# Two-layer recurrent attention on one core: first-step values, weight halves, transposes in steps 0, 1 and 67, and the order of the last dense tiles

## The chip, the cores and the metric

One core of a Trainium2 chip. The time is device microseconds for one execution of the program; the figure for a kernel is the median over its runs.

## The reference, cut to what matters

```python
def _A_ref(x, mem0, Wq, Wk, Wv, Wo, seg_len):     # S 2048, Dm 512, H 32, Dh 128, M 8, seg_len 32
    mem = mem0
    for s in range(n_seg):                        # 64 segments, each needs the memory of the one before
        xs = x[:, s * seg_len:(s + 1) * seg_len, :]
        h = concatenate([mem, xs], axis=1)        # 40 rows
        q, k, v = h @ Wq, h @ Wk, h @ Wv          # per head
        scores = where(mask, q @ k.T * scale, -1e9)
        o = (softmax(scores) @ v) @ Wo            # summed over heads
        mem = o[:, :M, :]
        outs.append(o[:, M:, :])
    return concatenate(outs, axis=1)

x = A_x
x = x + _A_ref(_layernorm(x), A_mem0, A_Wq, A_Wk, A_Wv, A_Wo, A_seg_len)
x = x + relu(_layernorm(x) @ B_w1) @ B_w2         # Dff 1376
x = x + _A_ref(_layernorm(x), A_mem0, A_Wq, A_Wk, A_Wv, A_Wo, A_seg_len)
x = x + relu(_layernorm(x) @ B_w1) @ B_w2
```

Both attention layers, and both dense layers, have the same weights. All arrays are bf16.

## The kernel before, in words

**Steps.** The work is cut into 68 steps (`LAST` = 67). Step k does segment k of the first attention layer (a = 0) and segment k - 4 of the second (a = 1, `DELTA` = 4), so that one load of a weight tile serves both layers. Steps 0 to 3 and 64 to 67 have one layer only. The two layers sit in partitions 0 to 39 and 64 to 103 of the score, P and value tiles.

**A step on TensorE (PE).** `qk(0)`: queries and keys of heads 0 to 15 (L467); scores of that half (L497); `qk(1)` and its scores for heads 16 to 31; P transposed, so that keys lie in partitions (first half: one DMA transpose, `turn_p`, or PE in `transpose_p`, L534); `weighted_v` (pv, L560); copies of pv into `OTm` (memory rows) and `OTx` (tokens), L577; `output_mem` (wo, L505), which gives the new memory; its copy wm, the transposes mt (L743) into `HT` and `HTm`; `memory_values` (vm, L636) for the next step. Work with no place in this chain fills gaps: `output_x(k - 1)`, the token outputs of the step before (wox, L327 with 64 rows, L348 with 32); the dense layer of tile d = k - 2 (`dense_h`, hp, L407; `dense_y`, sp, L427; `add_dense`; `store`); `values0`, the values of the next two segments of layer 0 (vp, L288, eight matmuls for each n of 0, 2, 4, 6); `values1` (L309). In steps with k % 4 == 0 ("ride" steps) the tokens of layer 0 go through the memory product in `OTm` and not through `OTx`.

**Values take a way through DRAM.** Heads have to move from the free dimension of a product into partitions of `Vs`; so values are written to DRAM (vst to vd, L297; VmS to vmd, L641) and read back (Vs<-vd, L620; Vs<-vmd, L646). In step 0 POOL's queue carries these DMAs, later SP's. A DMA that has to wait for another holds up all that stands behind it in its queue: in step 0 POOL has eight writes of vd, the read Vs<-vd, two writes of vmd, two reads Vs<-vmd, and behind these the multiply of the first half of P (L526).

**Order.** The orders of PE, VectorE (DVE), SP and POOL are the order in which the code records them (`manual_schedule`); high priority pulls the recurrent chain ahead. ScalarE's order is set by a scheduler.

**Start.** SP issues x0, x1, mem0, then the weights in quarters of 1 MB: Wq, Wk, Wq, Wk, Wv four times, Wq, Wk, Wq, Wk (L134) and Wo four times. Inputs are normalized (L219), transposed on PE (L230) and copied (L237). `HT` and `HTm` get the first memory at L772 and L773.

**End.** Segments 66 and 67 of layer 1 leave their rows in the second halves of tiles 66 and 67; dense tile 65 is done in step 67. Behind step 67 come `output_x(67)`, its adds (L362), the layer norm of the 128-row tile that holds both (bn_stats L786, normalize L219 into XN), its transposes (L230), the copy xnT (L790), hidden layer (hp), sums (sp), four adds (L798) and two DMAs.

**The clock.** PE's granted clock in the profile is 1.00 or 0.50.

Of the kernel before, what the change touches and what calls it, by code (L numbers as in the profile page):

```python
# [22 lines left out]
def kernel(  # L23
# [57 lines left out]
    def place1(s):  # L81
        if ride1(s):
            return s + 4, 32
        return s, (0 if s % 4 == 0 else 32)
# [23 lines left out]
    load_xb(1)  # L108
    nc.sync.dma_start(out=mem0[0:M, :], in_=A_mem0[0, :, :])
# [20 lines left out]
    PW = H * Dh // 4  # L130
# [4 lines left out]

    for pc in range(2):
        load_w(Wq_sb, Wq_v, pc)
        load_w(Wk_sb, Wk_v, pc)
    for pc in range(4):
        load_w(Wv_sb, Wv_v, pc)  # L140
    for pc in range(2, 4):
        load_w(Wq_sb, Wq_v, pc)
        load_w(Wk_sb, Wk_v, pc)
# [174 lines left out]
    def ox_span(k):  # L318
        offs = ([0] if has0(k) and not ride0(k) else [])
        if has1(k) and not ride1(k):  # L320
            offs.append(place1(k)[1])
        return (base(k) + min(offs), base(k) + max(offs) + 32) if offs else None
# [13 lines left out]
    def output_x(k, lo, hi):  # L336
        if not 0 <= k <= LAST or ox_span(k) is None:
            return
        r0, r1 = [x - base(k) for x in ox_span(k)]
        if lo == 0:  # L340
            pool, tag = (ps_wo, "wo") if k < LAST else (ps_fill, "fill")
            wo_tiles[k] = pool.tile([128, Dm], F32, tag=tag, name="wox")
        for h in range(lo, hi):
            if r1 - r0 == 64:
                halves(wo_tiles[k], OTx[:, h, r0:r1], Wo_sb[:, h, :], h == 0, h == H - 1)
            else:
                for j in range(4):
                    nc.tensor.matmul(wo_tiles[k][32 * j:32 * j + 32, 0:128], lhsT=OTx[:, h, r0:r1],  # L348
                                     rhs=Wo_sb[:, h, 128 * j:128 * j + 128], start=(h == 0), stop=(h == H - 1),
                                     tile_position=(0, 32 * j))  # L350
# [63 lines left out]
    def dense_y(d, f0, f1):  # L414
        if not 0 <= d <= LAST:
            return
        lo, hi = span(d)
        summed(d, f0, f1, hi - lo)

    def summed(d, f0, f1, n):  # L420
        for fc in range(f0, f1):
            fs = 128 if fc < NFC - 1 else F_LAST
            for j in range(2):


                w = 8 * L if fc == 0 else 256
                nc.tensor.matmul(sp_banks[1][64 * j:64 * j + n, 0:w], lhsT=hT_tiles[d][0:fs, fc, 0:n],  # L427
                                 rhs=w2_flat[0:fs, fc * Dm + 256 * j:fc * Dm + 256 * j + w],
                                 start=(fc == 0), stop=(fc == NFC - 1), skip_group_check=True, tile_position=(0, 64 * j))
# [71 lines left out]
    def output_mem(k, wo):  # L501
        n, c = divmod(k % 4, 2)
        for h in range(H):
            j = h % 4
            nc.tensor.matmul(wo[32 * j:32 * j + 32, :], lhsT=OTm[:, h, n, 2 * M * c:2 * M * c + 4 * M], rhs=Wo_sb[:, h, :],  # L505
                             start=(h < 4), stop=(h >= H - 4), tile_position=(0, 32 * j))

    def softmax(hf, act, meanwhile=lambda: None):
# [11 lines left out]
        meanwhile()  # L520
        for a, es in ess.items():
            sm = wk.tile([128, 8], F32, tag="sm", bufs=2)
            nc.vector.tensor_reduce(out=sm[:], in_=es[:], axis=AX.X, op=ALU.add)  # L523
            nc.vector.reciprocal(out=sm[:], in_=sm[:])  # L524
            eng = nc.vector if (hf, a) == (1, act[-1]) else nc.gpsimd
            eng.tensor_tensor(out=P_sb[:, :, 64 * a:64 * a + L], in0=es[:],  # L526
                              in1=sm[:].unsqueeze(2).to_broadcast([128, 8, L]), op=ALU.mult)
# [37 lines left out]
    def outputs(k, pvs):  # L565
# [7 lines left out]
        def copy(t, a, dst, lo, hi, parts=1):  # L573
            src = pvs[t, a][:, 0:PVS[t][1], lo:hi]
            if parts > 1:
                src = src.rearrange("p h (n t) -> p h n t", n=parts)
            engines[a if len(act) == 2 else t % 2](out=dst, in_=src)  # L577
# [16 lines left out]
        for a in act:  # L594
            for t in every:
                mem(t, a)
                if a == 0 and ride0(k):
                    quarter(t, 0)
            for t in every:
                if a == 0 and ride0(k):  # L600
                    quarter(t, 1)
                else:
                    tok(t, a)
# [47 lines left out]
    def block(k, lo, hi):  # L651
        output_x(k - 1, lo, hi)
        if k % 4 == 1 and has0(k + 1):
            p = (k + 1) // 2
            for n in range(0, NCH, 2):
                wo_bank = n == 0 or (n == 6 and k > 1)
# [4 lines left out]
    def step(k):  # L661
# [4 lines left out]
        has_x = n_x < NXT  # L666
        if k % 4 == 0 and has_x:
            load_xb(n_x)
# [7 lines left out]
        with tc.high_priority(offset=PRIO):  # L676
            load_values(k, act, q)
        if k == 0:
            with tc.high_priority(offset=PRIO):
                memory_values(0, q)  # L680
        part = 5 if len(act) == 2 else 8
        block(k, 0, part)
        with tc.high_priority(offset=PRIO):
# [3 lines left out]
            softmax(0, act)  # L687
            if k > 0:
                turn_p()
# [6 lines left out]
        if k == LAST - 2:  # L696
            for r in (0, 64):
                nc.gpsimd.memset(residual(LAST)[r:r + SEG, :], 0.0)
        with tc.high_priority(offset=PRIO):
            qks = qk(1, act)  # L700
        dense_h(k - 2)
        with tc.high_priority(offset=PRIO):
            scores(qks, act)
            if k == 0:
                softmax(1, act, lambda: transpose_p(0))
            else:
                softmax(1, act)
        block(k, part, 24 if k == 1 else H)
        ahead = has1(k + 1) or not cont
        f_mid = 9 if ahead else 5  # L710
        dense_y(k - 2, 0, f_mid)
# [5 lines left out]
        if ahead:  # L717
# [4 lines left out]
        with tc.high_priority(offset=PRIO):  # L722
            pvs = weighted_v(act)
            outputs(k, pvs)
            if cont:
                wo = ps_wo.tile([128, Dm], F32, tag="wo", name="wo")
                output_mem(k, wo)
                wm_sb = wm_tiles[k] = wk.tile([128, Dm], BF, tag="vst", bufs=5, name="wm")
                nc.scalar.copy(out=wm_sb[:], in_=wo[:])
        if k == 1:  # L730
            block(k, 24, H)
        if not ahead:
            dense_y(k - 2, f_mid, NFC)
        add_dense(k - 2)
        store(k - 2)
# [15 lines left out]
        if cont:  # L751
            output_ride(k)
            with tc.high_priority(offset=PRIO):
                memory_values(k + 1, nc.sync)
# [11 lines left out]
    with tc.manual_schedule(engines={mybir.EngineType.PE, mybir.EngineType.DVE, mybir.EngineType.SP,  # L766
# [14 lines left out]
        for k in range(LAST + 1):  # L781
            step(k)
        output_x(LAST, 0, H)
        add_output(LAST)
        R = residual(LAST)
        nc.vector.bn_stats(out=stats_all[:], in_=R[:])  # L786
        normalize(nc.vector, XN, R, stat_tail(stats_all), 0, 128)
        tp = transpose_pe(XN)
        xnT = wk.tile([128, NC4, 128], BF, tag="xnT", bufs=2, name="xnT")
        nc.scalar.copy(out=xnT[:], in_=tp[:])  # L790
        hidden(LAST, lambda c4: xnT[:, c4, :].rearrange("p (d t) -> p d t", d=2)[:, :, SEG:64], 64)
        summed(LAST, 0, NFC, 64)
        ob = wk.tile([128, Dm], BF, tag="ob", bufs=1, name="ob")
        for e in range(2):
            r = 64 * e + SEG
            for j in range(2):
                cs = slice(256 * j, 256 * j + 256)
                nc.vector.tensor_tensor(out=ob[r:r + SEG, cs], in0=R[r:r + SEG, cs],  # L798
                                        in1=sp_banks[1][64 * j + SEG * e:64 * j + SEG * e + SEG, 0:256], op=ALU.add)
            g = LAST - 1 + e - DELTA  # L800
            nc.sync.dma_start(out=out[0, SEG * g:SEG * g + SEG, :], in_=ob[r:r + SEG, :])
# [35 lines left out]
```

## Time and profile before

| what | value |
|---|---|
| median of 3 runs (1629.74, 1635.59, 1633.28) | 1633.28 us |
| profiled execution's own time | 1629.26 us |
| its span in the profile | 1627.5 us |
| granted PE clock, mean | 0.987 |
| PE busy / VectorE / ScalarE / POOL | 1569.9 / 1256.8 / 736.7 / 355.6 us |
| matmuls | 42966 |
| step 24 to step 63, each | 23.3 to 23.6 us, a few up to 0.7 longer |

The page has the busy time of each engine, the span in 40 slices (a digit is the busy share in tenths), the DMA queues, the chain of waits that ended last (shares by engine and by line), and the costliest groups of instructions. Each line of a timeline gives the start, the time, the engine, the line of the kernel, the operation with its tiles and shapes, the count of instructions run together, and in brackets the idle time before and what ended it.

### The profile page before, as it was taken

Reading aid. Unit: us, or ns where it says so; the run is one execution under the profiler, and the core shown is the slowest. Engines: PE = TensorE matmul, PEld = TensorE weight load, DVE = VectorE, ACT = ScalarE, POOL = GpSimd, SP = SyncE. Lnnn points to the kernel's source line nnn. Section 1 sums busy time; section 2 is a strip of 40 time slices with the busy share of each in tenths; the row PEclk is TensorE's granted clock in tenths of the full one; section 3 lists DMA queues with packets and bytes.
Section 4 is the critical chain, followed back from the end, with each engine's and each line's share of the span. In section 5 each row is a group of like instructions: output and inputs, shape, how many; then the busy total and the mean of one; then the engine's idle time right before and its main releaser. Section 6 shows DMA issues by size and latency. Waiting matters only on the chain.

```text
span 1627.5 us, 95385 instructions
## 1 busy us (share of the span) xinstructions
PE 1569.9 (96%) x42966; PEld 1327.6 (82%) x42966; DVE 1256.8 (77%) x3119; ACT 736.7 (45%) x1781; POOL 355.6 (22%) x683
## 2 busy tenths in 40 slices
PE   4789999999999999999999999999999999999997
PEld 2568888988888888889888888888888888888875
DVE  2467888888888887888888888878888887787764
ACT  2334445454444545454454445444444544444432
POOL 3111222222222222222222222222222221222110
PEclk8799999999999999999999999999999999999998
DMA  9634334543444334344343444444344344424331
GB/s 355 209 61 89 83 77 81 93 89 70 90 86 84 77 82 93 81 76 88 81 92 66 99 84 81 75 89 89 66 95 85 92 63 88 88 67 85 75 67 38
DMA packets 221800, 147.68 MB, mean 91 GB/s; under 512 B 127896, under 2 KB 211392, under 8 KB 220304
## 3 DMA queue, kind: packets, MB, share of 16 engines
q1 hardware_dynamic: 217856, 136.26, 38.9%
q8 instruction: 337, 5.52, 1.5%
q0 software_dynamic: 3536, 5.31, 1.3%
q14 instruction: 71, 0.58, 0.1%
HBM read 65.74 MB, written 45.61 MB: 68 GB/s over the span
## 4 chain that ended last, share of the span: by engine, by line
PE 94%; DMA 2%; issue 1%; ACT 1%; DVE 1%; SPq 1%; POOL 0%; POOLq 0%; DVEq 0%; ACTq 0%
PE qp L467 37%; PE wox L327 10%; PE wo L505 8%; PE vm L636 7%; PE v L309 7%; PE hp L407 6%; PE sp L427 5%; PE sp L497 4%; PE vp L288 4%; PE pv L560 3%; PE tp L534 1%; DMA Wv_sb<-in_A_Wv_dram 1%; PE wox L348 1%; PE xp L383 1%; SPq L134 1%
## 5 line engine op out<-in xcount | busy, mean ns | idle before, releaser
L471 ACT CAST QT<-qp 128x480 bf16<-128x480 f32 (+3 forms) x408 | 201.5, 494 | 397.5 <-PE qp L467 392.9
L467 PE MATMUL qp<-HT,Wq_sb 128*128 128x80 bf16 (+1 forms) x8704 | 370.8, 200 | 4.9 <-DMA Wq_sb<-in_A_Wq_dram 1.8
L467 PE MATMUL qp<-HT,Wk_sb 128*128 128x80 bf16 (+1 forms) x8704 | 369.7, 199 | 3.4 <-DMA Wk_sb<-in_A_Wk_dram 2.0
L467 PEld LDWEIGHTS <-Wq_sb 128*128 128x128 bf16 x8704 | 326.5, 99 | 36.8 <-issue 29.3
L467 PEld LDWEIGHTS <-Wk_sb 128*128 128x128 bf16 x8704 | 328.6, 100 | 4.3 <-DMA Wk_sb<-in_A_Wk_dram 2.3
L473 DVE CAST KT<-qp 128x480 bf16<-128x480 f32 (+3 forms) x408 | 225.3, 565 | 109.1 <-PE qp L467 106.9
L526 POOL TENSOR_TENSOR P_sb<-es,sm 128x320 bf16<-128x320 f32 x188 | 132.7, 719 | 792.3 <-DVE sm L524 583.2
L513 DVE TENSOR_REDUCE mx<-sp 128x8 f32<-128x320 f32 x256 | 115.0, 487 | 99.0 <-PE sp L497 99.0
L327 PE MATMUL wox<-Wo_sb,OTx 128*64 128x256 bf16 x2880 | 173.4, 273 | 0.0
L523 DVE TENSOR_REDUCE sm<-es 128x8 f32<-128x320 f32 x256 | 118.9, 465 | 44.7 <-ACT es L519 34.0
L327 PEld LDWEIGHTS <-OTx 128*64 128x64 bf16 x2880 | 150.2, 110 | 2.9
L636 PE MATMUL vm<-Wv_sb,HTm 128*32 128x512 bf16 x2176 | 137.2, 383 | 1.8 <-issue 1.1
L519 ACT ACTIVATE es<-es 128x320 f32<-128x320 f32 x256 | 110.8, 469 | 54.0 <-DVE es L517 52.3
L505 PE MATMUL wo<-Wo_sb,OTm 128*32 128x512 bf16 x2144 | 129.7, 384 | 2.3 <-ACT OTm L577 0.6
L309 PE MATMUL v<-Wv_sb,xnT 128*32 128x512 bf16 x2048 | 129.0, 378 | 0.0
L489 DVE CAST sp<-maskb 128x320 f32<-128x320 bf16 x256 | 118.4, 484 | 0.0
L636 PEld LDWEIGHTS <-HTm 128*32 128x32 bf16 x2176 | 88.8, 97 | 32.1 <-issue 13.5
L517 DVE TENSOR_TENSOR es<-sp,mx 128x320 f32<-128x320 f32 x256 | 113.8, 483 | 1.5
L427 PE MATMUL sp<-w_sb,hT 128*64 128x256 bf16 (+4 forms) x1474 | 106.8, 279 | 0.7 <-ACT hT L410 0.7
L640 ACT CAST VmS<-vm 128x512 bf16<-128x512 f32 x136 | 79.8, 586 | 55.4 <-PE vm L636 55.4
L407 PE MATMUL hp<-xnT,w_sb 128*128 128x64 bf16 (+3 forms) x2948 | 101.5, 194 | 1.3 <-ACT xnT L790 0.7
L407 PEld LDWEIGHTS <-w_sb 128*128 128x128 bf16 (+1 forms) x2948 | 95.6, 101 | 1.5 <-issue 1.5
(100 smaller groups left out, 2026.6 us busy)
## 6 DMA issues: line engine op xcount, KB each, us to landing
Vs<-vd SPq DMA_DIRECT2D x97, 256.0 KB
vmd<-VmS SPq DMA_DIRECT2D x134, 128.0 KB
vd<-vst SPq DMA_DIRECT2D x128, 128.0 KB
vd<-vst SPq DMA_DIRECT2D x128, 64.0 KB
Vs<-vmd SPq DMA_DIRECT2D x254, 32.0 KB
Vs<-vmd SPq DMA_DIRECT2D x60, 128.0 KB
Wq_sb<-in_A_Wq_dram SPq DMA_DIRECT2D x4, 1024.0 KB
Wk_sb<-in_A_Wk_dram SPq DMA_DIRECT2D x4, 1024.0 KB
```

The source lines that it names most:

```text
L309: nc.tensor.matmul(vp[32 * j:32 * j + 32, :], lhsT=xnT_tiles[s - 1][:, c4, r:r + SEG], rhs=Wv_sb[:, c4, n * 512:(n + 1) * 512], start=(c4 ...
L327: nc.tensor.matmul(out[64 * j:64 * j + nr, 0:256], lhsT=lhsT, rhs=rhs[:, 256 * j:256 * j + 256], start=start, stop=stop, tile_position=(0, ...
L407: nc.tensor.matmul(hp[0:fs, fc - f0, 0:n], lhsT=w1_sb[:, c4, fc * 128:fc * 128 + fs], rhs=cols(c4), start=(c4 == 0), stop=(c4 == NC4 - 1))
L427: nc.tensor.matmul(sp_banks[1][64 * j:64 * j + n, 0:w], lhsT=hT_tiles[d][0:fs, fc, 0:n], rhs=w2_flat[0:fs, fc * Dm + 256 * j:fc * Dm + 256 ...
L467: nc.tensor.matmul(qp[:, hi, 0:ncol], lhsT=W_sb[:, c4, h * Dh:(h + 1) * Dh], rhs=HT[:, c4, a_lo:a_hi, :], start=(c4 == 0), stop=(c4 == NC4 ...
L471: nc.scalar.copy(out=dst[:, 0:nh, a_lo * L:a_hi * L], in_=qp[:, 0:nh, 0:ncol])
L473: nc.vector.tensor_copy(out=dst[:, 0:nh, a_lo * L:a_hi * L], in_=qp[:, 0:nh, 0:ncol])
L489: nc.vector.tensor_copy(out=sp_tiles[a], in_=maskb2)
L505: nc.tensor.matmul(wo[32 * j:32 * j + 32, :], lhsT=OTm[:, h, n, 2 * M * c:2 * M * c + 4 * M], rhs=Wo_sb[:, h, :], start=(h < 4), stop=(h > ...
L523: nc.vector.tensor_reduce(out=sm[:], in_=es[:], axis=AX.X, op=ALU.add)
L526: eng.tensor_tensor(out=P_sb[:, :, 64 * a:64 * a + L], in0=es[:], in1=sm[:].unsqueeze(2).to_broadcast([128, 8, L]), op=ALU.mult)
L636: nc.tensor.matmul(vp[32 * j:32 * j + 32, :], lhsT=HTm[:, c4, :], rhs=Wv_sb[:, c4, n * 512:(n + 1) * 512], start=(c4 == 0), stop=(c4 == NC ...
```

## The change

1. *Weights.* Wq, Wk and Wv come in halves of 2 MB (six DMAs instead of twelve), in the order x0, Wq half, mem0, x1, Wk half, Wv halves, Wq half, Wk half; Wo stays in quarters.
2. *Segments 2 and 3 of layer 0.* Their values (`values0(1, n)`) were all computed in step 1, eight matmuls in each of four groups. Now n = 0 and 2 stand in step 0 before the second half's transposes of P, n = 4 stands in step 0 between heads 0 to 23 and 24 to 31 of `output_mem`, and only n = 6 stays in step 1.
3. *Memory values of segment 1* are computed in step 1 behind `qk(0)` instead of at the end of step 0. In step 0 the two writes vmd now stand ahead of the read Vs<-vd in POOL's queue.
4. *Steps 0, 1 and 67.* VectorE multiplies both halves of P (POOL did one), and PE transposes both halves (in steps 1 and 67 a DMA did one): 16 more transposes in each of steps 1 and 67.
5. *Dense tile 65* is taken out of step 67 and stands behind the last outputs: its hidden layer before their adds, its sums behind the layer norm's VectorE work, its adds and store behind the last transposes.
6. *The last tile.* Segments 66 and 67 of layer 1 both go to tile 66, rows 0 to 31 and 32 to 63, so the last tile has 64 rows, two adds and one DMA instead of 128, four and two, and the memset of the old one is gone. Its sums go to the other score bank.
7. *Copies of pv in ride steps with two layers.* For the first group of heads VectorE and ScalarE trade places, and the loop order is by group and not by layer.

The order of instructions on PE is otherwise as before. In all, PE has 32 more pairs of load and matmul, VectorE 10 fewer instructions, POOL 5 fewer, SP 5 fewer.

```diff
...
             return s + 4, 32
+        if s >= LAST - 1:
+            return LAST - 1, 32 * (s - LAST + 1)
         return s, (0 if s % 4 == 0 else 32)
...
     load_xb(0)
-    load_xb(1)
-    nc.sync.dma_start(out=mem0[0:M, :], in_=A_mem0[0, :, :])
     R_tiles = {}
...
     Wo_v = A_Wo.rearrange("h e d -> e h d")
-    PW = H * Dh // 4
+    PW = H * Dh // 2
     hh = H // 4
...
 
+    load_w(Wq_sb, Wq_v, 0)
+    nc.sync.dma_start(out=mem0[0:M, :], in_=A_mem0[0, :, :])
+    load_xb(1)
+    load_w(Wk_sb, Wk_v, 0)
     for pc in range(2):
-        load_w(Wq_sb, Wq_v, pc)
-        load_w(Wk_sb, Wk_v, pc)
-    for pc in range(4):
         load_w(Wv_sb, Wv_v, pc)
-    for pc in range(2, 4):
-        load_w(Wq_sb, Wq_v, pc)
-        load_w(Wk_sb, Wk_v, pc)
+    load_w(Wq_sb, Wq_v, 1)
+    load_w(Wk_sb, Wk_v, 1)
     for pc in range(4):
...
             offs.append(place1(k)[1])
-        return (base(k) + min(offs), base(k) + max(offs) + 32) if offs else None
+        r = base(place1(k)[0] if k == LAST else k)
+        return (r + min(offs), r + max(offs) + 32) if offs else None
 
...
             return
-        r0, r1 = [x - base(k) for x in ox_span(k)]
+        r0, r1 = [x % 64 for x in (ox_span(k)[0], ox_span(k)[1] - 1)]
+        r1 += 1
         if lo == 0:
-            pool, tag = (ps_wo, "wo") if k < LAST else (ps_fill, "fill")
-            wo_tiles[k] = pool.tile([128, Dm], F32, tag=tag, name="wox")
+            wo_tiles[k] = ps_wo.tile([128, Dm], F32, tag="wo", name="wox")
         for h in range(lo, hi):
...
 
-    def dense_y(d, f0, f1):
+    def dense_y(d, f0, f1, bank=1):
         if not 0 <= d <= LAST:
...
         lo, hi = span(d)
-        summed(d, f0, f1, hi - lo)
-
-    def summed(d, f0, f1, n):
+        n = hi - lo
         for fc in range(f0, f1):
...
                 w = 8 * L if fc == 0 else 256
-                nc.tensor.matmul(sp_banks[1][64 * j:64 * j + n, 0:w], lhsT=hT_tiles[d][0:fs, fc, 0:n],
+                nc.tensor.matmul(sp_banks[bank][64 * j:64 * j + n, 0:w], lhsT=hT_tiles[d][0:fs, fc, 0:n],
                                  rhs=w2_flat[0:fs, fc * Dm + 256 * j:fc * Dm + 256 * j + w],
...
 
-    def output_mem(k, wo):
+    def output_mem(k, wo, h0=0, h1=H):
         n, c = divmod(k % 4, 2)
-        for h in range(H):
+        for h in range(h0, h1):
             j = h % 4
...
 
-    def softmax(hf, act, meanwhile=lambda: None):
+    def softmax(hf, act, by_pe=False):
         mxs, ess = {}, {}
...
             nc.scalar.activation(out=es[:], in_=es[:], func=ACTF.Exp, scale=SCALE)
-        meanwhile()
+        if by_pe and hf:
+            transpose_p(0)
         for a, es in ess.items():
...
             nc.vector.reciprocal(out=sm[:], in_=sm[:])
-            eng = nc.vector if (hf, a) == (1, act[-1]) else nc.gpsimd
+            eng = nc.vector if by_pe or (hf, a) == (1, act[-1]) else nc.gpsimd
             eng.tensor_tensor(out=P_sb[:, :, 64 * a:64 * a + L], in0=es[:],
...
                 src = src.rearrange("p h (n t) -> p h n t", n=parts)
-            engines[a if len(act) == 2 else t % 2](out=dst, in_=src)
+            swap = ride0(k) and t == 0
+            engines[a ^ swap if len(act) == 2 else t % 2](out=dst, in_=src)
 
...
 
-        for a in act:
-            for t in every:
+        for t in every:
+            for a in act:
                 mem(t, a)
-                if a == 0 and ride0(k):
-                    quarter(t, 0)
-            for t in every:
+            if ride0(k):
+                quarter(t, 0)
+        for t in every:
+            for a in act:
                 if a == 0 and ride0(k):
...
         output_x(k - 1, lo, hi)
-        if k % 4 == 1 and has0(k + 1):
+        if k % 4 == 1 and k > 1 and has0(k + 1):
             p = (k + 1) // 2
             for n in range(0, NCH, 2):
-                wo_bank = n == 0 or (n == 6 and k > 1)
+                wo_bank = n in (0, 6)
                 for c4 in range(0, NC4, 2):
...
         has_x = n_x < NXT
+        by_pe = k in (0, 1, LAST)
         if k % 4 == 0 and has_x:
...
         with tc.high_priority(offset=PRIO):
-            load_values(k, act, q)
-        if k == 0:
-            with tc.high_priority(offset=PRIO):
-                memory_values(0, q)
+            if k == 1:
+                load_values(k, act, q)
+            if k < 2:
+                memory_values(k, q)
+            if k != 1:
+                load_values(k, act, q)
         part = 5 if len(act) == 2 else 8
...
             scores(qks, act)
-            softmax(0, act)
-            if k > 0:
+            softmax(0, act, by_pe)
+            if not by_pe:
                 turn_p()
...
             load_dense()
-        if k == LAST - 2:
-            for r in (0, 64):
-                nc.gpsimd.memset(residual(LAST)[r:r + SEG, :], 0.0)
         with tc.high_priority(offset=PRIO):
             qks = qk(1, act)
-        dense_h(k - 2)
+        if k < LAST:
+            dense_h(k - 2)
         with tc.high_priority(offset=PRIO):
             scores(qks, act)
-            if k == 0:
-                softmax(1, act, lambda: transpose_p(0))
-            else:
-                softmax(1, act)
-        block(k, part, 24 if k == 1 else H)
+            softmax(1, act, by_pe)
+        block(k, part, H)
+        if k == 0:
+            for n in (0, 2):
+                values0(1, n)
+        if k == 1:
+            values0(1, 6)
         ahead = has1(k + 1) or not cont
         f_mid = 9 if ahead else 5
-        dense_y(k - 2, 0, f_mid)
+        if k < LAST:
+            dense_y(k - 2, 0, f_mid)
         add_output(k - 1)
...
             transpose_p(1)
-        if ahead:
+        if ahead and k < LAST:
             dense_y(k - 2, f_mid, NFC)
...
                 wo = ps_wo.tile([128, Dm], F32, tag="wo", name="wo")
-                output_mem(k, wo)
+                if k == 0:
+                    output_mem(k, wo, 0, 24)
+                    values0(1, 4)
+                    output_mem(k, wo, 24)
+                else:
+                    output_mem(k, wo)
                 wm_sb = wm_tiles[k] = wk.tile([128, Dm], BF, tag="vst", bufs=5, name="wm")
                 nc.scalar.copy(out=wm_sb[:], in_=wo[:])
-        if k == 1:
-            block(k, 24, H)
         if not ahead:
             dense_y(k - 2, f_mid, NFC)
-        add_dense(k - 2)
-        store(k - 2)
+        if k < LAST:
+            add_dense(k - 2)
+            store(k - 2)
         values1(k + 1, 0)
...
             with tc.high_priority(offset=PRIO):
-                memory_values(k + 1, nc.sync)
+                if k > 0:
+                    memory_values(k + 1, nc.sync)
         if k < LAST:
...
             step(k)
+
+
         output_x(LAST, 0, H)
+        dense_h(LAST - 2)
         add_output(LAST)
-        R = residual(LAST)
-        nc.vector.bn_stats(out=stats_all[:], in_=R[:])
-        normalize(nc.vector, XN, R, stat_tail(stats_all), 0, 128)
+        d = LAST - 1
+        R = residual(d)
+        lo, hi = span(d)
+        nc.vector.bn_stats(out=stats_all[lo:hi, :], in_=R[lo:hi, :])
+        normalize(nc.vector, XN, R, stat_tail(stats_all), lo, hi)
+        dense_y(LAST - 2, 0, NFC)
         tp = transpose_pe(XN)
-        xnT = wk.tile([128, NC4, 128], BF, tag="xnT", bufs=2, name="xnT")
-        nc.scalar.copy(out=xnT[:], in_=tp[:])
-        hidden(LAST, lambda c4: xnT[:, c4, :].rearrange("p (d t) -> p d t", d=2)[:, :, SEG:64], 64)
-        summed(LAST, 0, NFC, 64)
-        ob = wk.tile([128, Dm], BF, tag="ob", bufs=1, name="ob")
-        for e in range(2):
-            r = 64 * e + SEG
-            for j in range(2):
-                cs = slice(256 * j, 256 * j + 256)
-                nc.vector.tensor_tensor(out=ob[r:r + SEG, cs], in0=R[r:r + SEG, cs],
-                                        in1=sp_banks[1][64 * j + SEG * e:64 * j + SEG * e + SEG, 0:256], op=ALU.add)
-            g = LAST - 1 + e - DELTA
-            nc.sync.dma_start(out=out[0, SEG * g:SEG * g + SEG, :], in_=ob[r:r + SEG, :])
+        add_dense(LAST - 2)
+        store(LAST - 2)
+        xnT_tiles[d + 2] = wk.tile([128, NC4, 128], BF, tag="xnT", bufs=2, name="xnT")
+        nc.scalar.copy(out=xnT_tiles[d + 2][:], in_=tp[:])
+        dense_h(d)
+        dense_y(d, 0, NFC, 0)
+        ob = wk.tile([128, Dm], BF, tag="xb", bufs=1, name="ob")
+        add_halves(ob[lo:hi, :], R[lo:hi, :], sp_banks[0])
+        nc.sync.dma_start(out=out[0, S - 2 * SEG:S, :], in_=ob[lo:hi, :])
```

## The prediction

> **What bounds the kernel now.** I read the page first: busy shares, the span in 40 slices, then the shares of the chain of waits.
>
> ```profile
> span 1627.5 us, 95385 instructions
> PE 1569.9 (96%) x42966; PEld 1327.6 (82%) x42966; DVE 1256.8 (77%) x3119; ACT 736.7 (45%) x1781; POOL 355.6 (22%) x683
> ...
> PE   4789999999999999999999999999999999999997
> ...
> PEclk8799999999999999999999999999999999999998
> ...
> DMA  9634334543444334344343444444344344424331
> ...
> PE 94%; DMA 2%; issue 1%; ACT 1%; DVE 1%; SPq 1%; POOL 0%; POOLq 0%; DVEq 0%; ACTq 0%
> ```
>
> TensorE sets the end from slice 4 to slice 39; only the two ends have room, where PE has holes and the clock dips. So I cut the ends out (table of busy time by stretch; columns: length, PE busy, PE loads, VectorE, ScalarE, POOL, granted clock, DMA share, GB/s):
>
> ```profile
> 20.00:40.00 20.00, 11.42 (x156) 5.18 (x156) 1.95 (x5) 4.58 (x9) 5.87 (x11) 0.74 1.06 389
> 40.00:60.00 20.00, 11.40 (x229) 7.05 (x229) 6.96 (x19) 3.89 (x11) 2.84 (x6) 0.57 0.73 214
> ...
> 1612.00:1628.00 16.00, 6.27 (x118) 5.00 (x106) 4.39 (x12) 1.57 (x4) 0.55 (x1) 0.66 0.03 8
> 800.00:894.00 94.00, 93.85 (x2568) 80.50 (x2564) 76.53 (x189) 44.90 (x109) 21.88 (x42) 1.00 0.40 83
> ```
>
> From 20 to 60 us PE is idle for 17 us: the weights arrive at 389 GB/s until about 53. In the middle (800 to 894) PE idles 0.15 in 94 us. From 1612 on it works 6.3 of 16 us, at clock 0.66.
>
> The timeline of the first step gives the order in which its last part becomes ready:
>
> ```profile
> 37.87 0.50 POOL L620 DMA_DIRECT2D Vs<-vd  x1 [5.74 <-DMA vd<-vst]
> 38.37 1.11 POOL L641 DMA_DIRECT2D vmd<-VmS  x2
> 44.81 1.15 POOL L646 DMA_DIRECT2D Vs<-vmd  x2 [5.34 <-DMA vmd<-VmS]
> 45.97 0.73 POOL L526 TENSOR_TENSOR P_sb<-es,sm 128x320 bf16<-128x320 f32 x1
> ```
>
> POOL waits 5.74 us for a round trip, only then sends the memory values (ready since VmS at 34.2), waits 5.34 us again, and only then multiplies P. On PE:
>
> ```profile
> 46.76 0.75 PE L534 MATMUL tp<-ident,P_sb 128*64 128x80 bf16 x16 [4.45 <-POOL P_sb L526]
> 49.48 0.74 PE L534 MATMUL tp<-ident,P_sb 128*64 128x80 bf16 x16 [1.98 <-DVE P_sb L526]
> 51.28 0.69 PE L560 MATMUL pv<-PT,Vs 40*128 40x40 bf16 x16 [1.05 <-DMA Vs<-vmd]
> ...
> 52.45 3.61 PE L505 MATMUL wo<-Wo_sb,OTm 128*32 128x512 bf16 x32
> ```
>
> The weighted values (pv) wait last for the memory values to return. The tail, on PE:
>
> ```profile
> 1616.35 0.40 PE L230 MATMUL tpx<-ident,XN 128*128 128x128 bf16 x4 [3.70 <-DVE XN L219]
> 1617.47 2.61 PE L407 MATMUL hp<-xnT,w_sb 128*128 128x64 bf16 x44 [0.72 <-ACT xnT L790]
> 1620.77 2.61 PE L427 MATMUL sp<-w_sb,hT 128*64 128x320 bf16 x22 [0.69 <-ACT hT L410]
> ```
>
> A 3.70 us hole while VectorE normalizes; at 1616.99 the granted clock falls to 0.5, and the two dense products take 2.61 us each.
>
> **The change part by part.**
>
> *Weights in halves, Wq's first.* The first Wq DMA is issued after one DMA instead of three: 2.14 to about 1.24, 0.9 us earlier. vd writes show a 4 KB packet at 167 ns, weights a 2 KB one at 86: 12.58 MB are 6144 x 86 / 16 = 33.0 us or 3072 x 167 / 16 = 32.1, so 0.96 less. Last Wk 39.85 to 38.0, last Wo 53.12 to 51.3. The Trainium skill ("DMA: Bandwidth & Descriptors", Specifications) gives about 358 GB/s as a core's limit from HBM; by it packet size would save nothing here and the sum below would be 1 us smaller. The trace moves 380 to 400 GB/s in most of this stretch, so no such limit shows.
>
> Price: mem0 and x1, landed at 3.4, now stand behind 2 MB of Wq, so about 9 (2 MB at 389 GB/s is 5.4 us behind a first packet near 2.3, plus their own). The first scores' operands move from 13.25 to about 16.6. Hidden: PE waits until 18.79 and again to 28.25 for Wv anyway (Wv now complete at 26.6); uncovered it would cost 3.4.
>
> *Memory values sent early.* Values of segments 0 and 1 from 20.8 to 30.0, memory values to 32.9, VmS 33.7; their two writes are issued at 32.4 to 34.3 instead of 38.37. With the 6.1 us that these writes and 6.3 that their return show, they are back at 45.3 to 47.2 instead of 51.15 to 51.76. P no longer waits on POOL: VectorE multiplies both halves (0.49 each). The second half's scores end at 42.4 as before (Wk 38.0, then 104 matmuls at some 33 ns, and 0.7), P at about 45.2 (42.35 plus max, subtract, exp, sum, reciprocal and product: 0.49, 0.49, 0.47, 0.48, 0.20, 0.49, plus gaps), its transposes to 46.0. So pv starts at 46.5 to 47.2, not 51.28; wo follows 1.2 us later as it does now. Its 24 heads at 0.113 us (cold) take 2.7, then 8 matmuls of values1 (1.9 cold, 1.05 warm), then the last 8 heads behind Wo at 51.3: wo ends at 51.8 (warm) to 53.3 (cold), before 56.06. Gain 2.8 to 4.3; I take 3.6, since PE is busy from 46.5 on and the clock should rise about 50.
>
> *Step 1.* Three of the four 8-matmul groups of segments 2 and 3 go to step 0's holes, two of them into the wait before transposes (cost nothing there: PE waits 4.45 and 1.98 us at them). In step 1 that saves 8 matmuls ahead of the scores (0.86) and some 0.4 in later waits; the multiply on VectorE ahead of two KT casts costs up to 0.49, and 16 more transposes (0.35 to 0.48) replace a DMA transpose, in the 1.52 us wait before the second transposes. Memory values move behind qk(0): 1.9 us, moved and not removed; the Vs path has about 2 us of room. Net +0.9. **Start 4.5** (bounds 2.4 and 6.5: below, cold throughout and step 1 nothing; above, warm and all of step 1's waits).
>
> *Ride steps.* In 15 steps pv's end to wo's start is 0.326 us against 0.107 elsewhere, so at most 15 x 0.22 = 3.3. The swap gives the chain's pair of copies (VectorE: 248 then 348 ns) to ScalarE, whose same shapes take 239 to 255 and 331: 0.03 a step. **0.5** (0 to 3.3).
>
> *Tail.* Dense 65 (1.33 + 1.2 us of PE) leaves the step; but PE there also stops for instructions: it resumes at 1598.54, 1602.56 and 1606.58, 4.02 us for each 128 pairs of load and matmul, and those stops take back most. VectorE's P, 16 more transposes and the four adds in line leave the last outputs 0.57 earlier. Then dense 65 runs in the 3.7 us hole at no cost. If PE stays warm, hp takes 1.33 instead of 2.61 and sp 1.3 instead of 2.61: 2.6. The last adds fall from four to two (1.73 to 0.86: 0.87; all rows are in two 0.43 us instructions). With 0.57 for the earlier outputs: **4.0** warm, 1.4 cold. Windows of the clock are 3.41 us long in the records, at a phase of their own; one with PE busy 0.54 was followed by half clock, one with 0.58 was not. In the new tail a window holds 1.7 to 2.6 us of PE work by its phase, 0.50 to 0.76 of its length (dense 65 from 1612.1, its second product about 1614.0 to 1615.3, the transposes 0.4, the last tile from 1616.9); by my drawing two phases in five come below 0.56. I take warm. The Trainium skill ("TensorE: Matmul & The Clock Gate", Part 1) says that half clock comes after at least one idle window. Read strictly, no window here would be idle and the tail would be 4.0 for certain; the 0.54 row speaks against reading it so.
>
> *At nothing:* the memsets of the last tile (POOL, far ahead of their use), the shorter SP queue (5 DMAs fewer), the seven rows POOL loses.
>
> Sum 4.5 + 0.5 + 4.0 = 9.0: the profiled execution (1629.26; span 1627.5) would be 1620.3. The median shown is 1633.28, 0.25% above that execution, so **1624**.
>
> **Rivals.**
> - *The tail goes cold:* 4.5 + 0.5 + 1.4 = 6.4, 1627. For it: busy share near the threshold. Against: PE has no hole over 0.7 us there.
> - *The start gives nothing:* the round trips lengthen under 4 KB packets (each of POOL's packets waits behind larger ones; vd's landing was 5.3 us under load), or Wo still ends it. 0 + 0.5 + 4.0: 1629. For it: DMA share 0.92 to 1.06. Against: 4 us of slack on POOL's order alone.
> - *The ride swap takes its whole wait:* 3.3 in place of 0.5: 1621.
> - *Slower: instruction blocks.* Step 1 has 16 more transposes and fewer values, so every later block of 128 pairs begins at another place. Where PE issues a pair in 25 ns (one-layer steps) it outruns the 4.02 us block and stops 0.3 to 1.8 us; in the two-layer steps the projections take 36 ns a pair, 4.6 us a block, and stops of 0.25 to 0.64 us stand in only five of 60 steps (the longest of the waits from 200 to 1500 us is 0.5, in this group). If the new phase puts one of 0.25 into every step, 60 x 0.25 = 15: 9 faster becomes 6 slower, 1639. It decides from 36 steps on. Against: 4.6 is above 4.02. The Trainium skill ("Runtime: NRT & Kernel Launch", Instruction fetch mechanics) calls crossing a 16 KiB block mostly hidden, which would strike this rival out; the stops at 1602 and 1605 (0.56 and 1.22 us) show that it isn't always.
>
> **How the numbers follow.** Forecast 0.43 (1624); cold tail 0.22 (1627); start nothing 0.17 (1629); whole ride wait 0.05 (1621); slower 0.13 (1639). The range takes all but the last: down to 1633.3 - 14.3 (6.5 + 3.3 + 4.5), less 2 us for the spread of the three runs (1629.74 to 1635.59), 1617; up to a gain of nothing with the same spread, 1635. About 0.3% (4.9 us) is what a measurement can tell from no change: faster below 1628.4. Faster is 0.43 + 0.05 + 0.8 of the cold tail + a quarter of the third: 0.69; slower 0.13; same 0.18.
>
> **What would show it.** Right: pv in step 0 near 47, memory values issued near 33; the swap leaves the steady steps at 23.3 to 23.6 us; hp and sp of the last tile at 1.3 us each, two last adds. Wrong: Vs<-vmd landing after 50; PE stops in the projections of most two-layer steps; the clock at 0.5 behind the last outputs; scores of step 0 later than the first Wv half.

## The result, and the profile after

The changed kernel takes 1621.44 us (median of 6 runs, 1618.67 to 1624.88), the kernel before 1633.26 (6 runs beside it, 1629.74 to 1635.59). The ratio is 0.9931 with a 95% interval of 0.9915 to 0.9947: some 11 us or 0.7% shorter, where 1624 was forecast. The profiled execution took 1618.67, its span 1617.0, against 1629.26 and 1627.5. From its page, the lines that answer to those of before:

```profile
span 1617.0 us, 95434 instructions
PE 1565.2 (97%) x42998; PEld 1322.3 (82%) x42998; DVE 1257.4 (78%) x3107; ACT 738.3 (46%) x1798; POOL 352.3 (22%) x678
...
PEclk9999999999999999999999999999999999999999
...
PE 92%; DVE 2%; SPq 2%; DMA 2%; issue 1%; ACT 1%; POOL 0%; POOLq 0%; DVEq 0%; ACTq 0%
```

PE is still the bound; the two low clock digits at the start are gone. VectorE has 12 instructions fewer (3119 to 3107), and not 10. Below, "warm" is a granted clock of 1.00 and "cold" one of 0.50. The stretches (columns as before; the tail has other limits, as the span is shorter):

```profile
20.00:40.00 20.00, 10.82 (x182) 6.08 (x179) 3.26 (x8) 4.57 (x9) 7.51 (x14) 0.86 1.03 403
40.00:60.00 20.00, 15.05 (x358) 10.28 (x358) 7.86 (x23) 6.09 (x16) 1.02 (x4) 0.80 0.78 214
...
1602.00:1617.00 15.00, 7.98 (x264) 6.85 (x264) 5.32 (x15) 2.25 (x7) 0.55 (x1) 0.93 0.03 9
```

POOL no longer waits before it sends the memory values, and pv comes five microseconds earlier (51.28 before):

```profile
33.00 0.54 POOL L643 DMA_DIRECT2D vmd<-VmS  x1 [0.37 <-ACT VmS L642]
37.25 0.51 POOL L622 DMA_DIRECT2D Vs<-vd  x1 [3.71 <-DMA vd<-vst]
38.20 0.60 POOL L648 DMA_DIRECT2D Vs<-vmd  x1 [0.43 <-DMA vmd<-VmS]
```

```profile
46.00 0.56 PE L560 MATMUL pv<-PT,Vs 40*128 40x40 bf16 x16
...
50.45 0.62 PE L504 MATMUL wo<-Wo_sb,OTm 128*32 128x512 bf16 x8 [2.32 <-DMA Wo_sb<-in_A_Wo_dram]
50.99 1.43 PE L288 MATMUL vp<-Wv_sb,xT 128*64 128x512 bf16 x8
53.29 1.04 PE L504 MATMUL wo<-Wo_sb,OTm 128*32 128x512 bf16 x8 [0.87 <-DMA Wo_sb<-in_A_Wo_dram]
...
1606.40 1.41 PE L426 MATMUL sp<-w_sb,hT 128*32 128x320 bf16 x22 [0.47 <-ACT hT L411]
1608.32 0.40 PE L230 MATMUL tpx<-ident,XN 128*128 128x128 bf16 x4 [0.51 <-DVE XN L219]
1609.43 1.51 PE L408 MATMUL hp<-xnT,w_sb 128*128 128x64 bf16 x44 [0.72 <-ACT xnT L809]
1611.63 1.42 PE L426 MATMUL sp<-w_sb,hT 128*64 128x320 bf16 x22 [0.69 <-ACT hT L411]
```

The first four lines belong to step 0: wo now waits for Wo twice, so 3.55 of pv's 5.28 us are lost again by mt (55.06 against 56.79). The last four are the tail: the hole ahead of tpx is 0.51 instead of 3.70, and the last products take 1.51 and 1.42 instead of 2.61 each.

To see where the time went I took the start of the mt transposes (those of the new memory), once a step, as milestones. The table has the two profiles of the changed kernel (the second is the run "again", below) less the profile of before; the last column is the forecast.

| stretch | first profile | second | forecast |
|---|---|---|---|
| first step, to its mt (56.79 before) | -1.73 | -1.89 | -3.6 |
| steps 1 to 3 | -1.41 | -1.82 | -0.9 |
| steps 4 to 63 | -1.35 | -2.05 | -0.5 |
| steps 64 to 66 | -1.81 | -0.88 | 0 |
| tail, to the end | -4.20 | -3.56 | -4.0 |
| sum | -10.5 | -10.2 | -9.0 |

The sum is near the forecast; three of its terms are not, and one of these, steps 64 to 66, is scatter (see the next run). That the sum came out near is in part luck.

### The profile page after: what moved, and what is told of

Read it like the earlier page. It is cut to its first block, busy times and chain, and to the rows that moved or that the text cites. A ratio compares the mean times of both kernels' runs of the same rounds, so it can differ in the third digit from the quotient of the medians.

```text
span 1617.0 us, 95434 instructions
## 1 busy us (share of the span) xinstructions
PE 1565.2 (97%) x42998; PEld 1322.3 (82%) x42998; DVE 1257.4 (78%) x3107; ACT 738.3 (46%) x1798; POOL 352.3 (22%) x678
## 4 chain that ended last, share of the span: by engine, by line
PE 92%; DVE 2%; SPq 2%; DMA 2%; issue 1%; ACT 1%; POOL 0%; POOLq 0%; DVEq 0%; ACTq 0%
PE qp L466 37%; PE wox L328 10%; PE wo L504 8%; PE vm L638 7%; PE v L309 7%; PE hp L408 5%; PE sp L426 5%; PE sp L496 4%; PE pv L560 4%; PE vp L288 3%; SPq L145 1%; PE tp L534 1%; DMA Wo_sb<-in_A_Wo_dram 1%; SPq L134 1%; PE xp L384 1%
```

## The experiments

All ratios are to the kernel before, from runs on the same chip.

| kernel | ratio, 95% interval | span of its profile |
|---|---|---|
| changed kernel | 0.9931, 0.9915 to 0.9947 | 1617.0 |
| noswap | 0.9929, 0.9913 to 0.9946 | 1619.8 |
| oldloop | 1.0090, 1.0075 to 1.0105 | 1645.8 |
| d65in | 0.9943, 0.9929 to 0.9958 | 1622.0 |
| vlate | 0.9943, 0.9920 to 0.9965 | 1620.2 |
| quart | 0.9934, 0.9914 to 0.9954 | 1616.9 |
| s1dma | 0.9960, 0.9944 to 0.9975 | 1624.2 |
| s1fill | 0.9942, 0.9926 to 0.9958 | 1617.2 |
| fill | 0.9910, 0.9895 to 0.9924 | 1614.8 |
| fill2 | 0.9913, 0.9898 to 0.9927 | 1613.3 |
| fill3 | 0.9915, 0.9900 to 0.9929 | 1618.2 |

### The same kernel once more

**again.** 

> The changed kernel itself, once more. Steps 1 to 3 took 61.0 us in its first profile and 58.6, 60.3 and 63.3 in three kernels that have the same instructions there; steps 64 to 66 took 60.5 and 62.4, 61.2, 60.4. Theory: what differs is the phase of clock windows and of instruction blocks in each execution, so this one also differs from its first profile by up to 2 us in either stretch, while the first step (to the first mt, 55.06) and the ride steps (23.41) repeat within 0.3 and 0.02. Rival: the same program repeats within 0.3 everywhere, and the differences come from the edits.

Measured: 1618.96 in its one run. First mt 54.90 (55.06), ride steps 23.41 (23.41). Steps 1 to 3 took 60.6 (61.0), steps 64 to 66 61.4 (60.5). So the first step and the ride steps repeat, as the theory had it, and steps 64 to 66 differ by 0.9. Over the eleven kernels below, which have the same PE instructions there, steps 64 to 66 ran from 60.1 to 63.1; before had 62.3. So the 1.8 us of the table's fourth row can't be put down to the change: the stops "issue" (PE waits for nothing that the profile shows) fall differently in each execution. Step 1 took 18.58 (18.42), but here the clock was 0.5 from 70.9 to 77.7, and wo and vm took longer than the 1.91 each of the first profile:

```profile
70.00 2.79 PE L504 MATMUL wo<-Wo_sb,OTm 128*32 128x512 bf16 x32
...
74.34 3.55 PE L638 MATMUL vm<-Wv_sb,HTm 128*32 128x512 bf16 x32 [0.15 <-PE xp L384]
```

### The copies of pv in ride steps

**noswap.**

```diff
-            engines[a ^ swap if len(act) == 2 else t % 2](out=dst, in_=src)
+            engines[a if len(act) == 2 else t % 2](out=dst, in_=src)
```

> The changed kernel with the new loop order of the copies, but without the trade of engines. Ride steps (k % 4 == 0) took 23.57 us before and 23.41 after, 15 x 0.16 = 2.4. Theory A, the loop order: before, the first matmul of wo in step 8 started at 234.222, 6 ns ahead of the end of ScalarE's 128x384 copy of layer-1 tokens (234.228) and 0.116 behind the end of VectorE's quarter (234.106), so ScalarE's signal sat on that long copy; the new order puts memory copies ahead of it. Then ride steps stay near 23.41 here and the total stays at the changed kernel's. Rival B, the trade: VectorE is held by PT_sb until 233.68, so giving its pair to ScalarE is what gains; then ride steps return to 23.57 and the total is 2.4 us longer.

**oldloop.** The loops of `outputs` are those of before, with `for a in act` outside; the trade stays.

> The changed kernel with the trade of engines in ride steps, but with the loop order of before (layer outside, group inside, tokens of layer 0 ahead of the memory rows of layer 1 in the record). Theory A (loop order): ride steps return to 23.57, the total is 2.4 us longer. Rival B (the trade): they stay near 23.41. If both this and the kernel without the trade stay at 23.41, either of the two is enough; if both return, both are needed.

Measured: ride steps took 23.57 without the trade, as rival B had it, though the median does not show the 2.4 us (0.9929). With the old loops they took 24.82 (some 26.49), which neither theory had. The three views show PE's waits for OTm from 140 to 1460 us: before, noswap, oldloop. The same view of the changed kernel has no wait for OTm.

```profile
PE wo L505 <- ACT OTm L577: 0.6, 4, 0.2
```

```profile
PE wo L504 <- ACT OTm L578: 0.9, 5, 0.2
```

```profile
PE wo L504 <- DVE OTm L578: 18.0, 13, 1.5
```

With the trade alone, VectorE does layer 1's first memory copy, and the old loops put it behind VectorE's six copies of layer 0: in step 8 it ends at 234.666 and wo follows at 234.781. The new loops put it first. That the trade needs the new loops is shown: without them it costs 25 us (medians of noswap and oldloop).

Why 0.16 and not 0.03? In step 8 of before, VectorE's quarter ends at 234.106 and wo loads at 234.222, 0.116 later; noswap has 0.115, oldloop's copy 0.115. In the changed kernel ScalarE's quarter ends at 230.835 and wo loads at 230.886, 0.051 later. In before and noswap PE has a separate semaphore instruction for VectorE (51 ns long) between the two; for ScalarE the load itself waits. So of the 0.14 us between before and the changed kernel by these rows (1.152 less 1.016 from the first pv to wo's load) 0.065 is a shorter release and 0.07 the quarter that ends earlier. The view names ScalarE as releaser for before, since its 128x384 copy ended at 234.228, later than the load began; I take the fixed distance to VectorE's end as the better reading, argued from four kernels and not tested by itself.

### The tail

**d65in.** `dense_h`, `dense_y`, `add_dense` and `store` of tile 65 go back into step 67.

> The changed kernel with dense tile 65 back in step 67 (hidden layer between the projections and the scores of the second half, sums ahead of the transposes); all else stays. Theory: the PE hole behind the last outputs comes back (3.7 us in before), one window of the clock is nearly idle, and the last tile's two dense products take 2.6 us each instead of 1.51 and 1.42: 2.3 us longer, plus up to 0.6 for the longer step 67, so 2 to 3 us in all. Rival: the clock stays warm without it, since the hole is shorter than a window of 3.41 us; then the last tile keeps 1.5 and 1.4 and the time is 0 to 0.6 us longer.

Measured: the span is 5.0 us longer than the changed kernel's, the ratio 0.0012 higher. Its tail, from the timeline of PE:

```profile
1604.60 1.86 PE L349 MATMUL wox<-Wo_sb,OTx 128*32 128x128 bf16 x120 [0.78 <-DVE OTx L578]
...
1610.83 0.61 PE L230 MATMUL tpx<-ident,XN 128*128 128x128 bf16 x4 [3.67 <-DVE XN L219]
1612.15 2.61 PE L408 MATMUL hp<-xnT,w_sb 128*128 128x64 bf16 x44 [0.72 <-ACT xnT L802]
1615.45 2.61 PE L426 MATMUL sp<-w_sb,hT 128*64 128x320 bf16 x22 [0.69 <-ACT hT L411]
```

The hole and the cold products are back. From the mt of step 66 to the end it takes 36.6, as before (36.3); the changed kernel 32.1. So in these profiles this part alone is the tail's gain: 4.5, of which 2.3 are the colder products, 1.5 the later outputs (19.2 from mt to the last outputs, against 17.7) and 0.6 a stop of PE and slower rows within them. The medians show 2 us of it, inside the intervals.

### What holds Wo back

**vlate.** All of `values0(1, ...)` in step 1, as in before.

> The changed kernel with all values of segments 2 and 3 in step 1 again, as before; memory values of segment 1 stay in step 1. After the change Wo's last quarter was there at 53.27, not at 51.3 as the forecast had it, though Wo's first packets came 1.8 us earlier. Theory C: the six 64 KB writes of these values, 0.4 MB or 1.1 us at 350 GB/s, share the last of Wo's time; without them Wo is complete near 52.2, and wo ends 1 us earlier or more, also because 8 matmuls no longer stand ahead of its last 8 heads. Rival D: Wo is held up by POOL's read-backs (from 41.5 to 46.0 only 661 packets of 1 KB pass where 1512 would at the rate around it); then Wo is complete at 53.2 here too and step 0 ends within 0.3 of the changed kernel. Either way step 1 gets longer by the three groups, 0.9 to 2 us, so the total is 0 to 2 us longer.

Measured: the last heads of wo start at 54.17, behind a wait of 2.59 for Wo. That is neither theory's time (52.2 or 53.2), and the run does not decide between them: with the six writes gone from SP's queue, SP issues the read Vs<-vd of step 1 (256 KB) at 47.98 and not behind them, and its 32 packets of 8 KB pass from 51.0 on among the last of Wo. In the changed kernel they pass from 55.5, behind Wo. First vlate's two rows, then the changed kernel's:

```profile
47.98 0.41 SPq L622 DMA_DIRECT2D Vs<-vd  x1
54.17 1.05 PE L504 MATMUL wo<-Wo_sb,OTm 128*32 128x512 bf16 x8 [2.59 <-DMA Wo_sb<-in_A_Wo_dram]
```

```profile
54.56 0.34 SPq L622 DMA_DIRECT2D Vs<-vd  x1
```

So theory C is not tested. The first mt comes at 55.95 (55.06), step 1 takes 21.24 (18.42 and 18.58); steps 2 and 3 give some of it back by chance. In the total a part of it shows at most.

**norb.** In step 0 `load_values` and `load_memory_values` are left out and Vs is zeroed at the start.

> The changed kernel without the read-backs of step 0: the values and memory values of the first segment are not loaded from DRAM, Vs is set to zero instead, so the first segment's outputs and all that hangs on them are left out. Theory D: these read-backs hold up Wo (1 KB packets fell to a third from 41.5 to 46.0 us); without them Wo's last quarter is complete at 50.5 to 51.8 and not 53.27, and wo ends that much earlier. Rival: the dip stays (the x rows for the residual, or the write of values, cause it) and Wo is complete at 53 or later.

Measured: the last heads of wo start at 51.31 and the first mt is at 52.66 (55.06), though Wk came 0.9 later:

```profile
49.69 1.05 PE L289 MATMUL vp<-Wv_sb,xT 128*64 128x512 bf16 x8
51.31 0.61 PE L505 MATMUL wo<-Wo_sb,OTm 128*32 128x512 bf16 x8 [0.57 <-DMA Wo_sb<-in_A_Wo_dram]
```

So theory D holds in that the read-backs cost Wo 2.0 us in the changed kernel, in one run, in which one load of 64 KB of x rows also left this stretch (issued at 33.97 and not at 39.51). It does not show that the change made it so. In the kernel before the same read-backs run into Wo too: its 1 KB packets fall from about 170 in half a microsecond to 13 at 42.5 and to 62 at 50.5. The large read Vs<-vd was issued at 37.87 before and at 37.25 after; only the small ones moved, from 44.81 to 38.20. What the read-backs cost before was not run, and why 0.3 MB cost so much stays open.

**quart.** `PW = H * Dh // 4`, each half as two DMAs in the same order.

> The changed kernel with Wq, Wk and Wv in quarters of 1 MB (2 KB packets) in the same order. Theory by packet times (86 ns for 2 KB, 167 for 4 KB): 12.58 MB take 0.96 us more, so the second Wk half is complete at 39.5 and not 38.6, and Wo 1 us later than 53.27; total 0.5 to 1 us longer. Rival: the rate is set elsewhere; Wk at 38.6 within 0.2 and the total unchanged. Finer pieces could also let the first projections start earlier, which the wait for Wv would hide.

Measured: the second Wk half is complete at 39.98 (38.62) and the first mt at 56.40 (55.06), so 1.3 us by smaller packets, or by the larger number of DMAs, which this run does not separate; the median hides it (0.9934). The Trainium skill ("DMA: Bandwidth & Descriptors", Specifications) has about 358 GB/s as a core's limit from HBM; here 403 GB/s came from 20 to 40 us with 4 KB packets and 391 in quart with 2 KB (389 before).

### The clock, and a faster version

**s1dma.** `by_pe = k in (0, LAST)`.

> The changed kernel with step 1 as before in P: POOL multiplies the first half, a DMA transposes it (steps 0 and 67 stay by PE). Theory: 16 transposes of 0.48 leave PE and stand in a wait otherwise, VectorE's two casts of keys are not held by 0.49; the Vs path and the DMA transpose have room; step 1 is within 0.5 of 18.4 us and the total is the same. Rival: the DMA transpose and POOL are late since the start is 1.7 us earlier and their loads are under way; then the second transposes or pv of step 1 wait for it and step 1 takes 0.5 to 2 us more. Steps 2 and 3 vary by 1 to 2 us in each execution, so the waits of step 1 decide and not the total.

Measured: 0.9960, slower than the changed kernel by 0.3% with intervals that just touch, a miss. Step 1 took 20.41 (18.42). Its PE rows:

```profile
70.11 0.74 PE L534 MATMUL tp<-ident,P_sb 128*64 128x80 bf16 x16 [2.38 <-DVE P_sb L526]
...
71.96 3.60 PE L504 MATMUL wo<-Wo_sb,OTm 128*32 128x512 bf16 x32
...
77.12 3.49 PE L638 MATMUL vm<-Wv_sb,HTm 128*32 128x512 bf16 x32 [0.15 <-PE xp L384]
```

The hole of 2.38 leaves PE 1.02 us of work in the 3.41 us before 70.12; then the clock is 0.5 until 80.4, and wo and vm run at half speed.

**s1fill.** s1dma, with twelve mask products whose result nobody reads ahead of the second `transpose_p` of step 1:

```diff
+    def warm(n):
+        for _ in range(n):
+            nc.tensor.matmul(sp_banks[1][:, 0:8 * L], lhsT=ident[:], rhs=maskb2, start=True, stop=True,
+                             skip_group_check=True)
```

> The kernel with step 1's P by POOL and DMA, and 12 of the unread mask products put into PE's hole ahead of step 1's second transposes (2.38 us long there). That kernel's median was 4 us above the changed kernel's, and in its profile wo of step 1 took 3.60 us and the memory values 3.49, where a warm execution has 1.91 each. Theory: the 16 transposes that the change puts on PE in step 1 earn their gain by keeping the clock's window busy; with the hole filled, wo and the memory values take 1.91 each and the ratio to before goes from 0.996 to about 0.994 or 0.993. Rival: the DMA transpose and POOL cost it elsewhere (loads, the Vs path); then the ratio stays near 0.996 though the clock is up.

Measured: wo and vm take 1.91 each, step 1 18.43, the ratio 0.9942. So what the 16 transposes give in step 1 is work in a hole: other work does it as well. This rests on one profile of each kernel (the intervals of the two ratios overlap), and the transposes don't always suffice: with them in place wo of step 1 took 2.79 in again and 3.36 to 3.56 in oldloop, norb and fill2, against 1.91 in five other profiles.

**fill.** The changed kernel with `warm(12)` and `warm(5)` ahead of heads 16 and 24 of wo in step 0, `warm(2)` and `warm(5)` around pv in step 67.

> The changed kernel with idle PE filled by products that nobody reads (the mask product of the start, 128x320): 12 ahead of heads 16 to 23 of wo in step 0, 5 ahead of its last 8 heads, 2 and 5 ahead of pv and of the last outputs in the tail. Theory: the clock decides. In the changed kernel 51.5 to 58.3 us ran at clock 0.5, and in the three other kernels with dense 65 behind the outputs the last outputs' 128 products took 3.48, 3.59 and 2.84 us where a warm execution took 1.97, as a window with holes of 0.4 to 0.8 us came before. With the holes filled, the projections of step 1 take 0.62 us a batch and not 0.8 (about 1 us earlier there) and the last outputs 2.0: 0.5 to 2 us shorter than the changed kernel. Rival: the holes are not what decides (the two stretches are cold here too), or the filling delays what stands behind it; then 0 to 1.5 us longer.

Measured: in its rows below, step 1's projections follow at 0.75 a batch (0.97 in the changed kernel); the last outputs take 1.97 at 1600.26. They take 1.97 in all three filled kernels; of the nine profiles with dense 65 behind the outputs and no filler there, seven have a cold window at these outputs (2.6 to 3.6 us). Median 1618.86, ratio 0.9910.

```profile
48.21 1.80 PE L665 MATMUL sp<-maskb,ident 128*128 128x320 bf16 x12
...
53.10 0.61 PE L504 MATMUL wo<-Wo_sb,OTm 128*32 128x512 bf16 x8 [0.29 <-DMA Wo_sb<-in_A_Wo_dram]
...
55.65 0.75 PE L466 MATMUL qp<-HT,Wk_sb 128*128 128x40 bf16 x24
```

**fill2.** fill, with `load_x(1)` and `load_x(2)` in step 1 and `add_output(66)` behind the copies of pv.

> The kernel with filled holes, and two more edits: the x rows of segments 1 and 2 for the residual (two 64 KB loads on POOL's queue at 39.5 and 43.1 us) are issued in step 1 behind the next step's tokens, and in step 67 the four adds of the outputs of step 66 (1.16 us of VectorE) stand behind the copies of pv, the last outputs in a bank of their own. Theory: without the two loads Wo's last quarter comes up to 0.7 earlier than 53.1 (without the read-backs too it came at 51.3), and PT_sb is no longer held by the adds (pv waited 0.4 to 0.6 for it), so the last outputs start 0.4 to 0.6 earlier: 0.4 to 1.3 us shorter than the filled kernel. Rival: the read-backs alone delay Wo (53.1 stays), and the adds, now ahead of the last outputs' own adds, give the time back; then the same within 0.3.

Measured: Wo's last wait ends at 52.80 (53.10), pv waits no more in step 67, but from mt to the end the tail takes 32.3 (32.1): the adds give it back and the stops for instructions stay. 0.9913, the same as fill, where 0.4 to 1.3 us less was expected.

**fill3.** fill2, with `warm(10)` ahead of step 1's second transposes.

> The changed kernel with filled holes, the two late loads and the late adds, and 10 unread mask products ahead of step 1's second transposes too (1.7 us hole there). Without them wo of step 1 ran at half clock in two of six profiles with these instructions (3.56 and 2.79 us against 1.91). Theory: it is now warm in all, the low runs stay and the high ones go: median 0.5 to 1 us below the filled kernels (ratio 0.990 to 0.991). Rival: the products push the transposes out (PE in order) and the gain is lost: ratio 0.9915 or above.

Measured: wo and vm of step 1 at 1.91, step 1 17.70; 0.9915. The ratio expected, 0.990 to 0.991, was missed: the gain is in the trace and not in the median. All three filled kernels lie below the changed kernel (0.9910 to 0.9915 against 0.9931), each by about the half width of an interval and none clear of it: probably 0.2% faster, not settled.

## Why the prediction was right

*Weights.* Right as a mechanism: first projections at 16.77 (16.6 forecast), Wv at 26.63 (26.6), Wk at 38.6 (38.0), the late memory load hidden. "Last Wo 53.12 to 51.3" failed: 53.27. Of the missing 2.0, Wk's lateness is 0.6, and four of the six 64 KB writes of the moved values now stand ahead of Wo's end: 0.26 MB, or about 0.75 us at 350 GB/s, an estimate that no run tests. The forecast has no term for these writes. The rest is open. Without read-backs Wo is there at 51.31 (norb), but the forecast had left them in, as in the kernel before.

*First step.* pv at 46.0 came half a microsecond ahead of the forecast (46.5 to 47.2), and the gain of 3.6 was wrong: 1.7 to 1.9, below the stated 2.8 to 4.3. The failed step is the sentence that the clock rises about 50 and the last heads stand behind Wo at 51.3. PE waited for Wo from 48.1 to 50.45 (1.09 us of work in the window 48.12 to 51.53), and the clock was 0.5 from 51.5 to 58.4. Wo is the larger part: with Wo at 51.31 the first mt came at 52.66 (norb), with the clock kept up at 54.45 (fill), against 55.06.

*Step 1.* -0.69 and -0.53 for -0.9. But I priced the 16 transposes as a small cost hidden in a wait; in s1dma, without them, the step ran cold and took 2.0 longer, and the median is some 4 us higher. Steps 1 to 3 together gained 1.4 to 1.8, but over all kernels here they ran from 58.6 to 63.8 (61.0), so the part beyond step 1 is scatter.

*Ride steps.* 0.5 forecast, 0.16 x 15 = 2.4 measured in these steps; other steps of the stretch took some of it back (1.35 and 2.05 are left in the table). The failed term is "0.03 a step": I counted the quarter's length and not the earlier start behind PT_sb and the release by the load's own wait. My bound of 3.3 held it.

*Tail.* 4.0 forecast, 4.2 and 3.6 measured, from terms that were off in both directions. Last outputs 1.7 earlier (19.44 to 17.74 from mt) and not 0.57: the instruction stops did not take dense 65 back. Products 2.2 to 2.3 (2.6). The last adds are 0.87 shorter, but only 0.24 is left at the end, as the one larger DMA follows the last add by 3.0 instead of 2.35 us.

*The rivals.* Cold tail: the last tile was warm in every profile with dense 65 behind the outputs. The cold window came earlier: in again and noswap the last outputs took 2.61 and 3.48 instead of 1.97, and so in seven of nine such profiles. So half of this rival is real, elsewhere, and the first profile, warm there too, was lucky. "The start gives nothing, or Wo still ends it": the second half of it was true, at a loss of some 1.9 and not of the whole 4.5. Slower by instruction blocks: no. Steps 42, 45, 47, 49 and 62 are 0.4 to 1.1 too long in the first profile; of these only step 45 is in the second, which has steps 38, 48, 56 and 58 instead, and before had 24, 43, 47 and 54. Nearly all of them move from execution to execution, so the code's position does not set them.

*The clock's rule.* I used "0.54 fell, 0.58 did not" as a threshold. Over the 14 profiles here, of the 3.41 us windows at full clock those with PE busy below 0.42 were all followed by half clock, those above 0.73 never, and between them either. A window already cold could be busy from end to end and be followed by another cold one (s1dma from 70.12, 3.41 of 3.41). My share of busy time alone is not what the clock goes by, and two in five was no better than a guess. The Trainium skill's idle window ("TensorE: Matmul & The Clock Gate", Part 1) cannot be read as an empty one: windows with 2.0 to 2.2 us of PE work were followed by half clock (noswap, vlate).

## What to carry to other kernels

Near a hole, ask of each filler or removed instruction what it does to the clock of the work behind it: in s1dma a hole of 2.4 us, left where 16 transposes of 0.5 us had been, went with products 3.3 us longer in all, and filled it went without. When a chain is shortened, look for what ends it next and what shares that resource: pv came 5.3 us earlier, but the last weights did not, and small transfers beside them cost 2.0. A trade of two engines has to be read together with the recorded order of each; alone it cost 25 us.

## What was not expected of the hardware

In step 8 a semaphore wait of PE in an instruction of its own released wo 0.115 us after the copy's end, one in the load itself 0.051. While POOL's read-backs (rows of 8 KB and 4 KB) and a load of x rows (2 KB) ran, the stream of 1 KB weight packets fell from about 170 to 14 to 101 in each half microsecond (41.5 to 45.5 us), and its packets took 54 to 118 ns instead of 52.
